# One-bank PSUM tiles from the second layer on, and the second layer's weights converted in the gated batches

## The chip, the cores and the metric

The kernel runs on one core of a Trainium2 chip. The metric is the device time of one execution in microseconds (us). A core has TensorE (PE: matmuls, with PEld for its weight loads), VectorE (DVE), ScalarE (ACT), GpSimd (POOL), and SyncE (SP), which issues nearly all DMA transfers here. Each engine works through its own instructions in the order in which they are written, and waits on semaphores where an operand is not ready or a buffer is not free.

## The reference

Three stages, each feeding the next (cut to the core):

```python
def _attn_ref(q, k, v, p):                       # batch 8, heads 8, seq 576, head_dim 64, 32 pack rows
    p_packed = sm_attn(p, k, v)
    return sm_attn(q, p_packed, p_packed)
def _moe_ref(x, w_gate, w_val, w_out, rms_g):    # 4608 tokens, 512 -> 1536 -> 512, "gated"
    xn = x / sqrt(mean(x * x) + 1e-6) * rms_g
    g = xn @ w_gate
    return silu(g) * (xn @ w_val) @ w_out
def _moe2_ref(x, w1, w2, w3, w_out):             # 512 -> 1024 -> 1024 -> 512, "second layer"
    return ((x @ w1) * (x @ w2) @ w3) @ w_out
```

q, k, v, p and rms_g arrive as fp32. The weight matrices arrive as 64-bit floats and are handed to the kernel as 64-bit words. The kernel turns each into fp32 on the core.

## The kernel before, in words

fp32 accuracy comes from splitting each operand into a high and a low part (`split`, line 54: ScalarE copies the rounded high part, VectorE or GpSimd subtracts) and adding three matmuls, high x high, high x low, low x high.

**Converting a weight.** `convert` (line 102) turns a block of 128 x 512 64-bit words into fp32: two activations on ScalarE (`c_h`, `c_y`), two VectorE instructions (`c_t`, `c_o`) and one GpSimd add. `converting` (line 116) is a generator over a list of such blocks: the first `next` issues the loads of the first few, each later `next` converts one block and issues one load. While the gated batches run three loads stand ahead, later two.

**Gated batches.** `dense_units(b)` (line 362) makes one of 8 batches: 6 groups x 2 x 2 halves x 2 units, so 48 units; a unit is 6 matmuls (line 376) into one `gv` bank. An even unit is drained by ScalarE (`th`, line 382) and VectorE (line 383), an odd one by ScalarE (`vl`, line 387); GpSimd multiplies them to `ht` (line 388), which SyncE stores to `hT_d`. There are four `gv` banks. After every eighth unit, `wb_unit` (line 330) makes the weights of the next group in an `at` tile, which ScalarE and VectorE split into `wbh` and `wbl`. `planned` (line 431) puts other work behind unit numbers: the attention of later batches (`pack`, `unpack`), and conversions. In batches 1 to 6 that is `some(ow, 2)` at units 21 and 35 (line 472), which converts the 12 blocks of `w_out` and stores them to `wo_d`.

**y stage.** `y_part(t)` (line 549) multiplies 512 tokens of `hT_d` by `w_out`: 12 units of 12 matmuls (line 558), into four banks named `at` or `gv` by turns. Beside them `together` (line 407) spreads other generators by due times: the conversions and splits of the second layer's `w3` and `w_out` and their product (`folded`, line 648), the Strassen parts of that product (`fold_parts`, line 665, stored to `w34_d`), and `layer2` (line 634). `layer2` converts four blocks of `w1` and `w2`, makes the operands of the group's seven Strassen products (seven block products in place of eight) in `group` (line 592: GpSimd adds, ScalarE and VectorE splits), and stores them to `ws_d`; then the next group. y_part 4 to 7 carry these, y_part 8 the preparation of the first token pair.

**Second layer.** Tokens go in five pairs of blocks, three of 2 x 512 and two of 2 x 384 columns (line 707). `run(p)` (line 915) first makes 8 `step`s (line 841): each is seven products of six matmuls (line 857) into four banks, `ta` to `td`, which VectorE and ScalarE combine as the products end. Then come the seven products with the folded weights (lines 941 to 951), with two sets of four banks, written in turns. Weights come from `ws_d` and `w34_d` through four buffers `w`.

**PSUM.** There are eight banks of 128 x 512 fp32. `bank()` gives one bank, tag `gv`, four buffers. `slot("at")` gives a tile of two banks, two buffers; the wide tiles are needed in the attention. `four(tag)` (line 538) returns four banks: four `gv` tiles, or the halves of two `at` slots. Even steps and the first set of products use `gv`, odd steps and the second set use `at` (lines 861 and 932). Waits are kept per tile: a matmul that starts to write one half of an `at` slot waits for readers of the other half as well.

```python
def four(tag):
    if tag == "gv":
        return [bank() for _ in range(4)]
    return [t[:, j, :] for t in (slot("at"), slot("at")) for j in range(2)]
```

Of the kernel before, what the change touches and what calls it, by code (L numbers as in the profile page):

```python
# [8 lines left out]
F32 = mybir.dt.float32  # L9
F32R = mybir.dt.float32r  # L10
I32 = mybir.dt.int32
# [13 lines left out]
NF = DFF // 128  # L25
# [7 lines left out]
def packed_attention_swiglu_bilinear(ctx: ExitStack, tc, qT, kT, v, pT, rms_g, w_gv, w_out,  # L33
                                     w1, w2, w3T, w_out2, out):
    nc = tc.nc
    PSUM = bass.MemoryType.PSUM

    const = ctx.enter_context(tc.tile_pool(name="const", bufs=1, side="left"))
    dram = ctx.enter_context(tc.tile_pool(name="dram", bufs=1, space=bass.MemoryType.DRAM))
    ps = ctx.enter_context(tc.tile_pool(name="ps", bufs=1, space=PSUM))  # L40

    hT_d = dram.tile([NF, 128, NT], F32, name="hT_d")
    wo_d = dram.tile([DFF, DM], F32, name="wo_d")
    w34_d = dram.tile([7, 128, 2, 4, 256], F32, name="w34_d")
    y_d = dram.tile([NT // TT, 128, 4, TT], F32, name="y_d")
    ws_d = [dram.tile([8, 128, 2, n, 2, 128], F32, name=f"ws{n}_d") for n in (3, 4)]

    def slot(tag):
        return ps.tile([128, 2, 512], F32, tag=tag, name=tag, bufs=2)

    def bank():
        return ps.tile([128, 512], F32, tag="gv", name="gv", bufs=4)
# [9 lines left out]
    cv = cv_ctx.enter_context(tc.tile_pool(name="cv", bufs=1, side="left"))  # L62
    cv_of = [cv]
# [52 lines left out]
    def converting(jobs, take):  # L116


        n64 = ahead64[0]
        ahead = [load64(src) for src, *_ in jobs[:n64]]  # L120
        yield
        for i, job in enumerate(jobs):
            take(ahead.pop(0), *job[1:])
            if i + n64 < len(jobs):
                ahead.append(load64(jobs[i + n64][0]))
            yield
# [4 lines left out]
    def as_f32(w):  # L131
        o = cv_of[0].tile([128, 512], F32, tag="c_o", name="c_o", bufs=c_o_bufs[0])
        convert(o, w, plain)
        return o
# [9 lines left out]
        store_later(4, out=dst, in_=as_f32(w))  # L144

    ahead64 = [3]


    pTs = att.tile([128, NC, B, NP], F32, name="pTs")
# [249 lines left out]
    def some(gen, n):  # L399
        for _ in range(n):  # L400
            yield next(gen, None)
# [5 lines left out]
    def together(main, total, *others, most=1):  # L407


        done, taken = 0.0, [0] * len(others)  # L410
        for c in main:
            done += c / total
            late = [n * (done - a) / (z - a) - taken[i] if taken[i] < n else 0.0
                    for i, (n, _, a, z) in enumerate(others)]
            for i in sorted(range(len(others)), key=lambda j: -late[j])[:most]:
                if late[i] > 0:
                    next(others[i][1], None)
                    taken[i] += 1
        for _, gen, _, _ in others:
            drain(gen)  # L420
# [37 lines left out]
            next(front[x])  # L458
    for x in "puw":
        drain(front[x])  # L460
    ow = converting([(w_out[128 * i:128 * i + 128, :], wo_d[128 * i:128 * i + 128, :]) for i in range(NF)], out_weight)

    PACK = [7, 7, 16, 31, 32, 40, 43]
    UNPACK = [0, 1, 3, 4, 6, 11, 13, 15, 17, 24, 24, 25, 31, 32, 40, 41, 42, 44]
    for b in range(B - 1):
        others = [(UNPACK, unpack(b + 1))]
        if b + 2 < B:
            others.insert(0, (PACK, pack(b + 2)))
        if b == 0:
            others.append(([1, 3, 5, 9, 12, 14, 18, 20, 22, 26, 28, 30], gvw))  # L470
        else:
            others.append(([21, 35], some(ow, 2)))
        planned(dense_units(b), *others)
    drain(ow)
    flush()
# [62 lines left out]
# [4 lines that stand above are left out]
# [41 lines left out]


    ORDER = (0, 5, 4, 1, 6, 3, 2)
    GROUPS = [(r, c) for c in range(2) for r in range(2)]
    parts = []

    def summed(w, g, n):
        parts.append(as_f32(w))  # L590

    def group(g):
        r, c = GROUPS[g]
        a11, a12, a21, a22 = parts
        parts.clear()
        to = stage[g % 2][:, :7168].rearrange("p (i j s n) -> p i j s n", i=4, j=7, s=2)

        def put(j, src, eng):
            hi, lo = (to[:, :, ORDER.index(j), s, :] for s in range(2))
            split(hi, lo, src.rearrange("p (i n) -> p i n", i=4), eng)  # L600

        put(3, a22, nc.vector)
        nc.gpsimd.tensor_tensor(out=a22, in0=a21, in1=a22, op=ALU.add)
        yield
        put(0, a11, nc.vector)
        nc.gpsimd.tensor_tensor(out=a21, in0=a11, in1=a21, op=ALU.subtract)
        nc.gpsimd.tensor_tensor(out=a11, in0=a22, in1=a11, op=ALU.subtract)
        yield
        put(4, a22, nc.vector)
        put(1, a12, nc.vector)  # L610
        nc.gpsimd.tensor_tensor(out=a12, in0=a12, in1=a11, op=ALU.subtract)
        yield
        put(6, a21, nc.vector)
        put(5, a11, nc.vector)
        yield
        put(2, a12, nc.vector)
        for i in range(4):
            store_later(2 + i, out=ws_d[0][4 * c + i, :, r], in_=to[:, i, :3].bitcast(F32))
            store_later(2 + i, out=ws_d[1][4 * c + i, :, r], in_=to[:, i, 3:].bitcast(F32))
        yield  # L620

    jobs = []
# [3 lines left out]
    for j in range(8):  # L626
        jobs.append((w3T[128 * j:128 * j + 128, 512:], w3_h[:, j], w3_l[:, j]))
    late = converting(jobs, halved)
    jobs = []
    for g, (r, c) in enumerate(GROUPS):  # L630
        for n, (w, kk) in enumerate(((w1, r), (w1, r + 2), (w2, r), (w2, r + 2))):
            jobs.append((w[128 * kk:128 * kk + 128, 512 * c:512 * c + 512], g, n))

    def layer2():
        conv = converting(jobs, summed)
        next(conv)
        yield
        for g in range(4):
            for _ in range(4):
                next(conv)  # L640
                yield
            yield from group(g)

# [66 lines left out]
    def fetch_y(p):  # L710
        if p < len(pairs):
            ys[p] = []
            row, w = pairs[p]
            for r in (row, row + w):
# [8 lines left out]

    second = layer2()
    third = fold_parts()
    together(y_part(4, "at"), 12.0, (6, some(second, 6), 0.5, 1.0), (5, some(third, 5), 0.0, 0.9))
    together(chained(y_part(5, "gv"), y_part(6, "at"), y_part(7, "gv")), 36.0, (31, second, 0.0, 0.9),
             (3, third, 0.0, 0.15),
             (1, (fetch_y(0) for _ in range(1)), 0.3, 0.4))

    flush()
# [93 lines left out]
             (3, first_w(), 0.3, 0.8))  # L825
    flush()
    wo_ctx.close()
    p3 = ctx.enter_context(tc.tile_pool(name="p3", bufs=1, side="left"))
    sides = {n: p3.tile([128, 4, TT], F32, name=n) for n in ("s11", "s21", "s12", "s22", "t1s", "t2s", "t4s")}
    OPER = {0: "s11", 4: "t1s", 5: "t2s", 1: "s21", 6: "s12", 3: "t4s", 2: "s22"}  # L830
# [10 lines left out]
    def step(p, n):  # L841
        w = width(p)
        i = LAYER[n]
        half, k = divmod(i, 4)
        xh, xl = xs[p]

        def side(name):
            return sides[name][:, k, :w]

        def prod(t, j, start):  # L850
            pos = ORDER.index(j)
            wi, pos, n = (wa, pos, 3) if pos < 3 else (wb_, pos - 3, 4)
            wi = wi[:, :512 * n].rearrange("p (r j s n) -> p r j s n", r=2, j=n, s=2)
            at = 0
            for a, x in ((0, xh), (1, xh), (0, xl)):
                for r in range(2):
                    nc.tensor.matmul(t, lhsT=wi[:, r, pos, a], rhs=x[:, j, r, :w],  # L857
                                     start=(start and at == 0), stop=(at == 5), skip_group_check=True)
                    at += 1

        ta, tb, tc_, td = (t[:, :w] for t in four("at" if n % 2 else "gv"))
        p1, u3, uc = tmp()[:, :w], tmp()[:, :w], two()
        u2, c22 = uc[:, 0, :w], uc[:, 1, :w]
        s1, s2 = (side("s21"), side("s22")) if half else (side("s11"), side("s12"))
        wa = next_w()
        prod(ta, 0, True)
        nc.scalar.activation(out=p1, in_=ta, func=AF.Copy)
        prod(tb, 5, True)
        dve(u2, tb, p1)
        prod(tc_, 4, True)  # L870
        yield
        wb_ = next_w()
        prod(ta, 1, False)
        prod(tb, 6, False)
        dve(u3, tb, p1)
        dve(c22, tc_, u3)
        yield
        prod(td, 3, True)
        dve(s1, td, u3)
        dve(s1, s1, ta, ALU.mult)  # L880
        prod(tc_, 2, False)
        dve(u2, tc_, u2)
        nc.gpsimd.tensor_tensor(out=s2, in0=u2, in1=c22, op=ALU.mult)  # L883
        if half == 0:
            diff(side("t1s"), s2, s1, nc.gpsimd)
        else:
            diff(side("t2s"), s2, side("t1s"), nc.gpsimd)
            diff(side("s12"), s2, side("s12"), nc.gpsimd)
            diff(side("t4s"), s1, side("t2s"), nc.gpsimd)
        yield  # L890
# [24 lines left out]
    def run(p):  # L915
        w = width(p)
# [12 lines left out]
        drain(diffs)  # L929
        later = splitting(p, LATER)  # L930
        sum_ = sums(p + 1)
        acc = [[t[:, :w] for t in four(tag)] for tag in ("gv", "at")]
        p1, u2, u3, c22 = [], [], [], []
        out_stores = []

# [5 lines left out]
        for a, j in enumerate(PROD):  # L941
            wi = next_w().rearrange("p (s i n) -> p s i n", s=2, i=4)
            last = {0: 1, 5: 6, 4: 2}.get(j, j) == j
            for k in range(4):
# [3 lines left out]
                for m in range(2):  # L948
                    t = acc[m][BANK[j]]
# [8 lines left out]
            for m in range(2):  # L958
                ta, tb, tc_, td = acc[m]
# [60 lines left out]
```

## Time and profile before

| | us |
|---|---|
| median of 3 runs (lowest, highest) | 1497.6 (1495.95, 1499.32) |
| the profiled execution | 1496.0 |
| its span, first to last instruction | 1494.2 |
| TensorE busy | 1360.8 (91%) |
| TensorE's share of the chain of waits that ended last | 72% of the span |
| VectorE busy | 871.6 (58%) |
| GpSimd busy | 607.0 (41%) |
| ScalarE busy | 576.5 (39%) |

Busy time is the time in which an engine executed something. Idle time stands in the groups of instructions: behind the second bar, the idle time of the engine just before these instructions, and what ended it. The stages lie in the span roughly so: attention of the first batches to 65, gated batches to 515, y stage to 866, second layer to the end.

### The profile page before, as it was taken

How to read it: one execution, taken by the hardware profiler on the slowest of the kernel's cores; microseconds unless marked ns; L12 is line 12 of the kernel's file. 1: busy time of each engine (PE TensorE's matmuls, PEld its weight loads, DVE VectorE, ACT ScalarE, POOL GpSimd, SP SyncE). 2: the span in 40 equal slices, each digit the busy share in tenths (PEclk: the TensorE clock that was granted, in tenths of full speed). 3: DMA queues.
4: the chain of work that ended last, by engine and by line, in shares of the span. 5: the costliest groups of instructions: out<-in, count | busy, mean ns of one | idle time of the engine just before them, and what ended most of it. 6: DMA issues, size and time to landing. Idle time of an engine off the chain costs nothing.

```text
span 1494.2 us, 23206 instructions
## 1 busy us (share of the span) xinstructions
PE 1360.8 (91%) x8800; PEld 1119.2 (75%) x8800; DVE 871.6 (58%) x1356; ACT 576.5 (39%) x1141; POOL 607.0 (41%) x524
## 2 busy tenths in 40 slices
PE   4579999999999999999899998998889889988888
PEld 2368888888888888888788776776667667878778
DVE  4786576676675577364786734654573447346344
ACT  3465554554556665252555410240042015014013
POOL 2455544545555622022344232452335326235233
PEclk9689999999999999999999999999999999999999
DMA  9844544433213577344899764465447545756654
GB/s 298 302 172 129 188 145 155 160 121 125 104 72 131 182 262 241 100 159 132 309 349 395 261 230 150 169 213 224 155 169 238 178 162 190 269 205 223 226 211 155
DMA packets 82080, 293.55 MB, mean 196 GB/s; under 512 B 9008, under 2 KB 14128, under 8 KB 68016
## 3 DMA queue, kind: packets, MB, share of 16 engines
q1 hardware_dynamic: 81968, 292.07, 56.4%
q8 instruction: 69, 1.13, 0.3%
q14 instruction: 43, 0.35, 0.1%
HBM read 219.68 MB, written 72.35 MB: 195 GB/s over the span
## 4 chain that ended last, share of the span: by engine, by line
PE 72%; DVE 13%; ACT 4%; DMA 3%; issue 3%; SPq 1%; POOL 0%; DVEq 0%; ACTq 0%; POOLq 0%
PE gv L376 17%; PE at L857 12%; PE gv L857 10%; PE at L558 9%; PE at L951 5%; PE gv L951 5%; PE gv L558 4%; PE gv L654 3%; DVE hr L839 3%; DVE uc L839 2%; PE at L337 2%; DMA w<-in_w_dram 1%; DMA hr<-hT_d 1%; PE at L292 1%; DVE s L839 1%
## 5 line engine op out<-in xcount | busy, mean ns | idle before, releaser
L388 POOL TENSOR_TENSOR ht<-th,vl 128x288 f32<-128x288 f32 x192 | 163.6, 861 | 166.7 <-ACT vl L387 79.3
L857 PE MATMUL at<-xh,w 128*128 128x512 f32 (+1 forms) x560 | 146.2, 383 | 56.1 <-DVE uc L839 28.1
L376 PE MATMUL gv<-ah,wbh 128*128 128x288 f32 x768 | 178.0, 313 | 7.3 <-DVE th L383 4.7
L883 POOL TENSOR_TENSOR s<-uc 128x512 f32<-128x512 f32 (+1 forms) x40 | 48.5, 1214 | 313.8 <-DVE uc L839 313.8
L376 PE MATMUL gv<-al,wbh 128*128 128x288 f32 x768 | 166.8, 298 | 0.0
L857 PEld LDWEIGHTS at<-xh,w 128*128 128x128 f32 x560 | 98.9, 189 | 90.2 <-DVE uc L839 35.7
L376 PEld LDWEIGHTS gv<-ah,wbh 128*128 128x128 f32 x768 | 122.3, 190 | 58.5 <-issue 22.8
L376 PE MATMUL gv<-ah,wbl 128*128 128x288 f32 x768 | 165.0, 296 | 0.0
L114 POOL TENSOR_TENSOR c_o<-c_o,c_y 128x512 int32<-128x512 int32 x52 | 74.4, 1431 | 173.0 <-DVE c_o L112 152.3
L857 PE MATMUL gv<-xh,w 128*128 128x512 f32 (+1 forms) x560 | 140.4, 372 | 3.4 <-DVE uc L839 2.2
L56 DVE TENSOR_TENSOR hl<-hr,hh 128x512 fp32r<-128x512 f32 x108 | 98.9, 919 | 49.5 <-ACT hh L55 49.3
L376 PEld LDWEIGHTS gv<-al,wbh 128*128 128x128 f32 x768 | 124.7, 190 | 1.0 <-DVE al L56 0.6
L376 PEld LDWEIGHTS gv<-ah,wbl 128*128 128x128 f32 x768 | 124.3, 190 | 0.0
L857 PEld LDWEIGHTS gv<-xh,w 128*128 128x128 f32 x560 | 101.4, 188 | 23.5 <-DVE uc L839 11.0
L383 DVE SCALAR_TENSOR_TENSOR th<-th,gv 128x288 f32<-128x288 f32 x192 | 84.4, 445 | 55.9 <-ACT th L382 52.1
L558 PE MATMUL at<-hl,wo_h 128*128 128x512 f32 x288 | 112.6, 391 | 2.3 <-DVE hl L56 2.3
L558 PE MATMUL at<-hh,wo_h 128*128 128x512 f32 x288 | 112.4, 390 | 0.2 <-ACT hh L55 0.2
L558 PE MATMUL at<-hh,wo_l 128*128 128x512 f32 x288 | 112.3, 390 | 0.0
L55 ACT ACTIVATE hh<-hr 128x512 fp32r<-128x512 f32 x108 | 67.5, 628 | 97.1 <-PE at L558 49.9
L387 ACT ACTIVATE vl<-gv 128x288 f32<-128x288 f32 x192 | 79.5, 414 | 62.1 <-PE gv L376 58.5
L56 DVE TENSOR_TENSOR wbl<-at,wbh 128x512 fp32r<-128x512 f32 x96 | 66.0, 687 | 61.2 <-ACT wbh L55 60.6
L951 PE MATMUL at<-sh,w 128*128 128x512 f32 (+1 forms) x280 | 83.9, 381 | 13.1 <-DVE uc L839 12.4
(148 smaller groups left out, 2828.0 us busy)
## 6 DMA issues: line engine op xcount, KB each, us to landing
w<-ws_d SPq DMA_DIRECT2D x40, 1024.0 KB, 4.8
w<-w_d SPq DMA_DIRECT2D x35, 1024.0 KB, 4.8
w<-ws_d SPq DMA_DIRECT2D x40, 768.0 KB, 4.4
hT_d<-ht SPq DMA_DIRECT2D x96, 288.0 KB, 2.6
hr<-hT_d SPq DMA_DIRECT2D x108, 256.0 KB, 5.3
w<-in_w_gv_dram SPq DMA_DIRECT2D x24, 512.0 KB, 7.2
w<-in_w_out_dram SPq DMA_DIRECT2D x20, 512.0 KB, 4.8
v<-in_v_dram SPq DMA_DIRECT2D x8, 1152.0 KB, 8.1
```

What stands on the lines that cost most here:

```text
L55: nc.scalar.activation(out=hi, in_=src, func=AF.Copy)
L56: eng_lo.tensor_tensor(out=lo, in0=src, in1=hi.bitcast(F32), op=ALU.subtract)
L114: nc.gpsimd.tensor_tensor(out=d, in0=d, in1=shape(y), op=ALU.add)
L376: nc.tensor.matmul(t[:, :HALF], lhsT=w[:, e, 256 * i + 128 * f:256 * i + 128 * f + 128], rhs=x[:, e, HALF * hf:HALF * hf + HALF], start=(n ...
L383: nc.vector.scalar_tensor_tensor(out=th, in0=th, scalar=1.0, in1=t[:, :HALF], op0=ALU.add, op1=ALU.mult)
L387: nc.scalar.activation(out=vl, in_=t[:, :HALF], func=AF.Copy, scale=0.5)
L388: nc.gpsimd.tensor_tensor(out=ht[:, hf], in0=th, in1=vl, op=ALU.mult)
L558: nc.tensor.matmul(acc[m], lhsT=w[:, kk, 128 * m:128 * m + 128], rhs=x, start=(kk == 0 and a == 0), stop=(kk == NF - 1 and a == 2))
L839: nc.vector.tensor_tensor(out=out, in0=a, in1=b, op=op)
L857: nc.tensor.matmul(t, lhsT=wi[:, r, pos, a], rhs=x[:, j, r, :w], start=(start and at == 0), stop=(at == 5), skip_group_check=True)
L883: nc.gpsimd.tensor_tensor(out=s2, in0=u2, in1=c22, op=ALU.mult)
L951: nc.tensor.matmul(t, lhsT=wi[:, s, k, 128 * m:128 * m + 128], rhs=x, start=(j in (0, 5, 4, 3) and k == 0 and n == 0), stop=(k == 3 and n ...
```

## The change

It has three parts.

1. The two-bank slots move to a pool of their own, which is closed before the second layer. In its place a pool `pt` gives four one-bank tiles `at`, and odd steps and the second set of products take these. The number of banks is the same.
2. The 16 blocks of `w1` and `w2` join the list of `w_out`'s 12. In batches 1 to 6 five places (units 9, 20, 28, 35 and 46) take the place of two, and the finished fp32 blocks are stored to a new DRAM tile `w12_d`.
3. `layer2` no longer converts. `fetch_part` loads a finished block; even groups go to the `c_o` buffers, odd groups in pairs to `w64` buffers. The seven steps of `fold_parts` all run beside y_part 4 (before: five there, the other two beside y_part 5).

```diff
+    w12_d = dram.tile([16, 128, 512], F32, name="w12_d")
+    slots_ctx = ExitStack()
+    slots = slots_ctx.enter_context(tc.tile_pool(name="slots", bufs=1, space=PSUM))
     def slot(tag):
-        return ps.tile([128, 2, 512], F32, tag=tag, name=tag, bufs=2)
+        return slots.tile([128, 2, 512], F32, tag=tag, name=tag, bufs=2)
...
-    ow = converting([(w_out[128 * i:128 * i + 128, :], wo_d[128 * i:128 * i + 128, :]) for i in range(NF)], out_weight)
+    jobs = [(w_out[128 * i:128 * i + 128, :], wo_d[128 * i:128 * i + 128, :]) for i in range(NF)]
+    for n in range(16):
+        r, c = GROUPS[n // 4]
+        w, kk = ((w1, r), (w1, r + 2), (w2, r), (w2, r + 2))[n % 4]
+        jobs.append((w[128 * kk:128 * kk + 128, 512 * c:512 * c + 512], w12_d[n]))
+    ow = converting(jobs, out_weight)
...
-            others.append(([21, 35], some(ow, 2)))
+            others.append(([9, 20, 28, 35, 46], some(ow, 5)))
...
-    def summed(w, g, n):
-        parts.append(as_f32(w))
+    def fetch_part(n):
+        if n < 16:
+            cv = cv_of[0]
+            if n // 4 % 2 == 0:
+                x = cv.tile([128, 512], F32, tag="c_o", name="c_o", bufs=4)
+            else:
+                if n % 2 == 0:
+                    two_parts.append(cv.tile([128, 512, 2], I32, tag="w64", name="w64", bufs=3))
+                x = two_parts[-1].rearrange("p n t -> p (n t)").bitcast(F32)[:, 512 * (n % 2):512 * (n % 2) + 512]
+            nc.sync.dma_start(out=x, in_=w12_d[n])
+            parts.append(x)
...
     def layer2():
-        conv = converting(jobs, summed)
-        next(conv)
+        for n in range(4):
+            fetch_part(n)
         yield
         for g in range(4):
-            for _ in range(4):
-                next(conv)
+            for n in range(4):
+                fetch_part(4 * g + 4 + n)
                 yield
             yield from group(g)
...
-    together(y_part(4, "at"), 12.0, (6, some(second, 6), 0.5, 1.0), (5, some(third, 5), 0.0, 0.9))
+    together(y_part(4, "at"), 12.0, (6, some(second, 6), 0.5, 1.0), (7, third, 0.0, 0.9))
     together(chained(y_part(5, "gv"), y_part(6, "at"), y_part(7, "gv")), 36.0, (31, second, 0.0, 0.9),
-             (3, third, 0.0, 0.15),
              (1, (fetch_y(0) for _ in range(1)), 0.3, 0.4))
...
     wo_ctx.close()
+    slots_ctx.close()
+    pt = ctx.enter_context(tc.tile_pool(name="pt", bufs=1, space=PSUM))
+
+    def banks(n):
+        if n % 2:
+            return [pt.tile([128, 512], F32, tag="at", name="at", bufs=4) for _ in range(4)]
+        return four("gv")
...
-        ta, tb, tc_, td = (t[:, :w] for t in four("at" if n % 2 else "gv"))
+        ta, tb, tc_, td = (t[:, :w] for t in banks(n))
...
-        acc = [[t[:, :w] for t in four(tag)] for tag in ("gv", "at")]
+        acc = [[t[:, :w] for t in banks(m)] for m in range(2)]
```

**TensorE, an odd step of the second layer.** Six matmuls (x1, x3, x2 in the rows) make one product, in the order `ta`, `tb`, `tc_`, then the second product into `ta`. In brackets stand the semaphores that the row waits for: DMAHW is a transfer's landing, Activation is ScalarE's count, DVE VectorE's. Before:

```order
L857 MATMUL at<-xh,w 128x512 [waits DMAHW6_49]
L857 MATMUL at<-xh,w 128x512 x3
L857 MATMUL at<-xl,w 128x512 x2
L857 MATMUL at<-xh,w 128x512 [waits Activation_49]
L857 MATMUL at<-xh,w 128x512 x3
L857 MATMUL at<-xl,w 128x512 x2
L857 MATMUL at<-xh,w 128x512 x4
L857 MATMUL at<-xl,w 128x512 x2
L857 MATMUL at<-xh,w 128x512 [waits DMAHW7_49,DVE_49]
```

The changed kernel:

```order
L879 MATMUL at<-xh,w 128x512 [waits DMAHW6_49]
L879 MATMUL at<-xh,w 128x512 x3
L879 MATMUL at<-xl,w 128x512 x2
L879 MATMUL at<-xh,w 128x512 x4
L879 MATMUL at<-xl,w 128x512 x2
L879 MATMUL at<-xh,w 128x512 x4
L879 MATMUL at<-xl,w 128x512 x2
L879 MATMUL at<-xh,w 128x512 [waits DMAHW7_49,Activation_49]
L879 MATMUL at<-xh,w 128x512 x3
L879 MATMUL at<-xl,w 128x512 x2
L879 MATMUL at<-xh,w 128x512 [waits DVE_49]
```

The wait for ScalarE's copy of `ta` has moved from the second product (into `tb`) to the fourth (into `ta` again), and the wait for VectorE's read of `tb` from the fourth to the fifth (into `tb` again).

**ScalarE, around unit 9 of a gated batch.** `e` is attention work, `th` and `vl` drain units 8, 9, 10 and 11, `wbh` splits the next group's weights, and the `th` and `vl` behind it drain units 12 and 13. Before:

```order
L188 ACTIVATE e_2429,rs<-at,nb 128x576 x2
L382 ACTIVATE th<-gv 128x288
L387 ACTIVATE vl<-gv 128x288
L382 ACTIVATE th<-gv 128x288
L387 ACTIVATE vl<-gv 128x288
L55 ACTIVATE wbh<-at 128x512 x2
L382 ACTIVATE th<-gv 128x288
L387 ACTIVATE vl<-gv 128x288
```

The changed kernel:

```order
L193 ACTIVATE e_2469,rs<-at,nb 128x576 x2
L387 ACTIVATE th<-gv 128x288
L392 ACTIVATE vl<-gv 128x288
L112 ACTIVATE c_h<-w_1981 128x512
L113 ACTIVATE c_y<-w_1981 128x512
L387 ACTIVATE th<-gv 128x288
L392 ACTIVATE vl<-gv 128x288
L59 ACTIVATE wbh<-at 128x512 x2
L387 ACTIVATE th<-gv 128x288
L392 ACTIVATE vl<-gv 128x288
```

The two activations of a conversion stand now between the draining of unit 9 and that of unit 10.

**SyncE, beside y_part 4 and the start of y_part 5.** `hr` are the rows of `hT_d` that y_part multiplies, `w_d<-stage` are stores of the folded weights, `in_w_dram` are 64-bit blocks of `w1` or `w2`. Before:

```order
L489 DMA hr<-hT_d 128x512
L99 DMA w_8505<-in_w_dram 128x1024
L99 DMA w_8507<-in_w_dram 128x1024
L489 DMA hr<-hT_d 128x512
L99 DMA w_8536<-in_w_dram 128x1024
L489 DMA hr<-hT_d 128x512 x2
L356 DMA w_d<-stage_6932 128x2048
L99 DMA w_8586<-in_w_dram 128x1024
L489 DMA hr<-hT_d 128x512
```

The changed kernel, where `c_o` and `w` are filled from `w12_d` and `ws_d` is the first store of group 0:

```order
L607 DMA c_o<-w_d 128x512 x4
L499 DMA hr<-hT_d 128x512 x2
L361 DMA w_d<-stage_7128 128x2048
L607 DMA w_8751<-w_d 128x512
L499 DMA hr<-hT_d 128x512
L607 DMA w_8751<-w_d 128x512
L499 DMA hr<-hT_d 128x512 x2
L607 DMA w_8816<-w_d 128x512 x2
...
L361 DMA ws_d<-stage_7127 128x768
```

Before, loads of 64-bit blocks are spread, two ahead of their conversion. Now the blocks of group 0 are loaded together, and those of group 1 before group 0's results are stored.

## Rows read from the trace of the kernel before

**Rows 1.** Groups by line: shapes, count | busy us, mean ns | idle before, releasers.
```profile
L857 PE MATMUL at<-xh,w 128*128 128x512 f32 (+1 forms) x560 | 146.2, 383 | 56.1 <-DVE uc L839 28.1 <-DVE s L839 14.6 <-ACT hr L867 13.5
L857 PE MATMUL gv<-xh,w 128*128 128x512 f32 (+1 forms) x560 | 140.4, 372 | 3.4 <-DVE uc L839 2.2
...
L951 PE MATMUL at<-sh,w 128*128 128x512 f32 (+1 forms) x280 | 83.9, 381 | 13.1 <-DVE uc L839 12.4
```

**Rows 2.** TensorE's timeline, two steps of 512 columns: start, us, instructions [idle before].
```profile
1002.82 1.09 PE L857 MATMUL gv<-xh,w 128*128 128x512 f32 x4
...
1012.83 1.07 PE L857 MATMUL at<-xh,w 128*128 128x512 f32 x4
...
1015.05 1.20 PE L857 MATMUL at<-xh,w 128*128 128x512 f32 x4 [0.69 <-ACT hr L867]
...
1022.30 1.21 PE L857 MATMUL at<-xh,w 128*128 128x512 f32 x4 [1.51 <-DVE uc L839]
...
1026.25 1.07 PE L857 MATMUL gv<-xh,w 128*128 128x512 f32 x4
```

**Rows 3.** TensorE's timeline, two steps of 384 columns.
```profile
1276.03 0.86 PE L857 MATMUL gv<-xh,w 128*128 128x384 f32 x4
...
1283.81 0.85 PE L857 MATMUL at<-xh,w 128*128 128x384 f32 x4
...
1294.43 0.86 PE L857 MATMUL gv<-xh,w 128*128 128x384 f32 x4
```

**Rows 4.** Busy us by stretch: PE, PEld, DVE, ACT, POOL, clock, DMA.
```profile
866.00:961.00 95.00, 82.36 (x343) 62.94 (x342) 42.72 (x57) 9.37 (x17) 30.00 (x22) 1.00 0.53 194
961.00:1003.00 42.00, 38.82 (x163) 30.12 (x162) 28.45 (x28) 21.87 (x33) 28.20 (x16) 1.00 0.60 199
```

**Rows 5.** The page's DMA issues: count, size, us to landing.
```profile
w<-ws_d SPq DMA_DIRECT2D x40, 1024.0 KB, 4.8
...
w<-ws_d SPq DMA_DIRECT2D x40, 768.0 KB, 4.4
```

**Rows 6.** TensorE's timeline, a stop in the folded products.
```profile
978.64 0.73 PE L951 MATMUL at<-sh,w 128*128 128x512 f32 x2 [1.66 <-DVE uc L839]
```

**Rows 7.** Chain of waits, y stage: start, us, what.
```profile
548.08 32.64 PE gv L558 x144
...
689.73 10.94 PE at L558 x48
...
716.97 7.00 DMA w<-in_w_dram
...
731.09 1.77 DVE hl L56
...
865.71 6.86 PE gv L857 x30
```

**Rows 8.** Busy us by stretch, around the stop in y_part 5, columns as above.
```profile
730.00:735.00 5.00, 2.12 (x6) 1.71 (x6) 5.00 (x5) 3.02 (x5) 3.63 (x3) 0.70 0.81 333
735.00:740.00 5.00, 5.00 (x15) 3.92 (x15) 4.41 (x6) 1.67 (x3) 1.48 (x2) 0.61 0.63 197
```

**Rows 9.** Groups by line: the instructions of a conversion.
```profile
L114 POOL TENSOR_TENSOR c_o<-c_o,c_y 128x512 int32<-128x512 int32 x52 | 74.4, 1431 | 173.0 <-DVE c_o L112 152.3 <-ACT hh L55 10.6 <-ACT c_h L108 9.0
...
L108 ACT ACTIVATE c_h<-w 128x512 f32<-128x512 f32 x76 | 50.7, 667 | 20.3 <-DMA w<-in_w_gv_dram 9.4 <-DMA w<-in_w_dram 4.5 <-DMA w<-in_w_out_dram 3.8
...
L111 DVE TENSOR_SCALAR c_t<-c_h 128x512 int32<-128x512 int32 x76 | 43.6, 573 | 25.1 <-ACT c_h L108 24.1
...
L112 DVE SCALAR_TENSOR_TENSOR c_o<-c_h,c_t 128x512 int32<-128x512 int32 x52 | 38.5, 740 | 1.8
```

**Rows 10.** Timeline of ScalarE and of TensorE, batch 4 at units 13 and 16.
```profile
324.71 0.42 ACT L387 ACTIVATE vl<-gv 128x288 f32<-128x288 f32 x1
...
325.18 0.54 PE L376 MATMUL gv<-ah,wbh 128*128 128x288 f32 x2 [0.29 <-ACT vl L387]
```

**Rows 11.** VectorE's low parts in the y stage: ns min/median/max, first and last start.
```profile
L56 DVE TENSOR_TENSOR hl<-hr,hh x108: 677/693/2785, 511.7 to 858.2; 128x512 fp32r<-128x512 f32 x108
```

More of the change, by code (lines that the diff above doesn't have):

```diff
@@ L146, in packed_attention_swiglu_bilinear @@
     ahead64 = [3]
+    GROUPS = [(r, c) for c in range(2) for r in range(2)]
     pTs = att.tile([128, NC, B, NP], F32, name="pTs")
@@ L585, in packed_attention_swiglu_bilinear @@
     ORDER = (0, 5, 4, 1, 6, 3, 2)
-    GROUPS = [(r, c) for c in range(2) for r in range(2)]
     parts = []
-    def summed(w, g, n):
-        parts.append(as_f32(w))
+    def fetch_part(n):
[9 more added lines that the diff above has]
+            parts.append(x)
+    two_parts = []
     def group(g):
         r, c = GROUPS[g]
-        a11, a12, a21, a22 = parts
-        parts.clear()
+        a11, a12, a21, a22 = parts[:4]
+        del parts[:4]
         to = stage[g % 2][:, :7168].rearrange("p (i j s n) -> p i j s n", i=4, j=7, s=2)
@@ L628, in packed_attention_swiglu_bilinear @@
     late = converting(jobs, halved)
[L629 to L632, printed above, removed]
     def layer2():
-        conv = converting(jobs, summed)
-        next(conv)
+        for n in range(4):
+            fetch_part(n)
         yield
         for g in range(4):
-            for _ in range(4):
-                next(conv)
+            for n in range(4):
+                fetch_part(4 * g + 4 + n)
                 yield
```

## The prediction

> **What bounds the kernel now.** I read the busy line and the 40 slices of the page first: TensorE is busy 91% of the span at nearly full granted clock, and the chain of waits is TensorE for 72%. So only TensorE's own stops can be won, or lengthened. The groups by line show where it stops [rows 1]: in line 857, the products of the second layer, the instructions that write tiles `at` stood idle 56.1 us ahead of their matmuls, the equal number that write `gv` 3.4 us; in line 951, the products with the folded weights, `at` stood 13.1 us. The two do the same arithmetic with the same operands and take turns, step by step. They differ only in the tile: a `gv` is one bank, an `at` is half of a tile of two banks, and the releasers named (the `uc`, `s` and `hr` that read the neighbour bank) are waits on the tile and not on the data.
>
> The timeline of TensorE then gives the price [rows 2]. A `gv` step of 512 columns runs from 1002.82 to 1012.83, 10.01 us; the `at` step behind it to 1026.25, 13.42 us, with stops such as 0.69 and 1.51 us. The rest of the 3.41 us is the restart, since the first four matmuls after a stop take 1.20 instead of 1.07 us and their predecessors drain first. For 384 columns [rows 3] it is 7.78 us (1276.03 to 1283.81) and 10.62 us (to 1294.43).
>
> In the stage before (y_part 4 to 8) the chain of waits runs from 689.73 to 865.71, 176.0 us [rows 7]. One y_part at full rate is 32.64 us, five are 163.2, so 12.8 us are lost there. [...]
>
> **The change part by part. One-bank tiles.** In the order of TensorE the `at` step now has the waits of a `gv` step: the wait for ScalarE has gone from the second product to the fourth, two products later than the read it waits for, and the wait for VectorE has gone from the fourth to the fifth. So I price an `at` step as a `gv` step. There are 5 pairs of token blocks with 4 `at` steps each, 3 pairs of 512 and 2 of 384 columns: 12 x 3.41 = 40.9 and 8 x 2.84 = 22.7, together 63.6 us. All of it lies on the path, since TensorE is the engine that ends last. What else must keep up: between 866 and 961 VectorE was busy 42.7, GpSimd 30.0 and ScalarE 9.4 of 95 us [rows 4]; the same work in about 81 us (14 less, four `at` steps) leaves VectorE half idle. The weights: a step loads 1024 and 768 KB, which land 4.8 and 4.4 us after issue [rows 5]; one after the other 9.2 us, which is under a `gv` step of 10.0 us and over one of 7.8, but three loads stand ahead in four buffers, so they may overlap. Nothing for it, and 16 x (9.2 - 7.78) = 22.7 us if they do not.
>
> In line 951 the `at` stops go as well: the fourth of seven products waited 1.66 us for VectorE's read of the bank beside it [rows 6]. There are about four such stops a pair, 13.1 us idle in all [rows 1], and 0.10 us more for each restart (0.73 instead of 0.63 us for two matmuls), 20 of them: 15 us. This stretch is fuller: between 961 and 1003 VectorE and GpSimd are busy 28.4 and 28.2 of 42 us [rows 4], and the splits that feed TensorE have six buffers. If they become the limit, I get perhaps 5 us of it; with the restarts fully counted 17. I take 15.
>
> **The conversions leave the y stage.** Sixteen times two activations, two VectorE instructions and one GpSimd add go, and 16 loads of 512 KB become 16 of 256 KB of finished fp32. No ScalarE instruction there waits any longer for a load issued shortly before: the order of SyncE shows the four loads of a group issued before the previous group is split. I take 9 of the 12.8 us; the rest I leave, because part of the stops late in the stage are behind stores that stay. The two fold steps that moved into y_part 4 bring two instructions on ScalarE and two on VectorE forward, with two units of `hl` ready ahead. Bounds: 0 (the stops are the loads' `hr` and stores alone, and come back there) and 12.8.
>
> **The conversions enter the gated batches.** One conversion is `c_h` and an equal `c_y` on ScalarE, 0.67 us each, `c_t` 0.57 and `c_o` 0.74 on VectorE, the add 1.43 on GpSimd [rows 9]. On a free engine nothing of this is late; on the queues the instructions behind it are. In the batches now two conversions stand, behind units 21 and 35 of 48; now five, behind 9, 20, 28, 35 and 46. The place without slack is 9: TensorE's unit 16 starts at 325.18, ended by ScalarE's `vl` that starts at 324.71 [rows 10]. The order of ScalarE shows the new pair just ahead of two `th`/`vl` and the `wbh` pair that this `vl` stands behind, so 2 x 0.67 = 1.3 us go through. The five conversions at this place are in batches 2 to 6 (batch 1 only begins the loads there): 6.5 us. At 20, 28 and 46 banks come free two or more units before they are wanted; half a microsecond in all. I take +7. Bounds: 0, if the chain closes up before unit 16; 16 x 1.33 = 21 if every conversion passes its ScalarE time on. The 16 extra stores and 16 loads of SyncE stand among the `hT_d` stores; the loads are three conversions ahead.
>
> [...] Row first: VectorE's `hl` takes 0.693 us in the median and up to 2.785 [rows 11], in the stage where GpSimd's adds run beside it. [...]
>
> **Sum.** 63.6 + 15 + 9 - 7 = 80.6 us. The profiled execution before took 1496.0 us (span 1494.2 and 1.8 around it), which gives 1415.4; the median of the three runs, 1497.6, stands 1.6 above it, so 1417; I write 1416.
>
> **Rivals.**
> - The folded products are held by VectorE and GpSimd (5 instead of 15 us): 1426. For it: 28 of 42 us busy on both engines [rows 4]. Against: every stop named there is `at` waiting for a read.
> - The y stage gives nothing: 1425. For it: TensorE's late stops there have other causes as well. Against: the load of 7.00 us and the conversion are in the chain of the largest one [rows 7].
> - The 384-column steps are held by the weights: 1416 + 23 = 1439. Against: no idle time of line 857 names a load [rows 1].
> - GpSimd's adds hold up VectorE in the batches, each for its 1.43 us, and TensorE behind it: 16 x 1.43 = 23 us, 1439. [...]
> - Each added conversion holds TensorE for its whole chain, 0.67 + 0.57 + 0.74 + 1.43 = 3.4 us, 54 instead of 7: 1463. Against: nothing TensorE needs waits for the add.
> - The new tiles wait as before (the order of banks brings other waits): 63.6 and 15 are not won, 1495, no change. Against: the order.
> - Slower: the 64-bit loads come late in the batches, behind SyncE's `hT_d` stores, and ScalarE's whole queue stands at `c_h` for a load of 7.0 us as at 717 [rows 7], then the chain of 3.4: 16 x 10.4 = 166 instead of 7, 1575. It makes the kernel slower from (63.6 + 15 + 9) / 16 = 5.5 us per conversion. Against: a load is issued three conversions ahead of its use.
>
> **How the numbers follow.** Forecast 0.70; folded products held 0.10; y stage nothing 0.08; weights 0.03; adds 0.02; whole chain 0.03; waits as before 0.02; slower 0.02. The forecast's own terms run from 63.6 + 17 + 12.8 - 0 = 93.4 (1404) to 63.6 + 12 + 4 - 14 = 66 (1431). The range 1404 to 1434 holds these and the first two rivals, both together too (1435) but for a microsecond. A measurement of this kernel can tell 0.2%, 3 us, from no change. Faster by more 0.96, within it 0.02, slower 0.02.
>
> **What would show it.** The `at` and `gv` groups of the second layer's products have the same idle time, under 5 us each, and an `at` step lasts 10.0 and 7.8 us; line 951 shows under 4 us of idle time. The stage of y_part 4 to 8 takes 165 to 170 us with no granted clock under 0.9 in a slice. The gated batches 2 to 6 are each about 1.3 us longer than now, with the extra stop at unit 16. I am wrong if steps of 384 columns show waits for `w`, if the splits `sl` become the releaser in the folded products, or if batches grow by more than 3 us each.

## The result, and the profile after

The changed kernel took 1410.7 us (median of 4 runs, 1409.9 to 1412.1) against 1498.4 us of the kernel before in the same comparison: a ratio of 0.9418, with a 95% interval of 0.9402 to 0.9434. The forecast was 1416 us and its range 1404 to 1434. The profiled execution has a span of 1408.3 us, 85.9 less than before.

The groups by line of the kernel after (shapes, count, then busy us and mean ns, then idle time ahead and who ended it) answer to [rows 1]; line 857 is now 879, and 951 is 973:

```profile
L879 PE MATMUL gv<-xh,w 128*128 128x512 f32 (+1 forms) x560 | 140.6, 372 | 3.4 <-DVE uc L861 2.8
L879 PE MATMUL at<-xh,w 128*128 128x512 f32 (+1 forms) x560 | 140.4, 372 | 3.4 <-DVE uc L861 2.5
L973 PE MATMUL at<-sh,w 128*128 128x512 f32 (+1 forms) x280 | 81.9, 374 | 0.0
```

The `at` instructions of the steps now wait as long as the `gv` ones, 3.4 us over 560 matmuls, and those of the folded products wait for nothing. TensorE's timeline (start, us, instructions, idle time before) shows two steps of 512 columns, as [rows 2], and then two of 384, as [rows 3]:

```profile
981.63 1.07 PE L879 MATMUL gv<-xh,w 128*128 128x512 f32 x4
...
990.10 1.21 PE L879 MATMUL gv<-xh,w 128*128 128x512 f32 x4 [0.15 <-DVE uc L861]
...
991.61 1.09 PE L879 MATMUL at<-xh,w 128*128 128x512 f32 x4
...
1000.11 1.20 PE L879 MATMUL at<-xh,w 128*128 128x512 f32 x4
...
1001.60 1.09 PE L879 MATMUL gv<-xh,w 128*128 128x512 f32 x4
```

```profile
1227.96 0.85 PE L879 MATMUL at<-xh,w 128*128 128x384 f32 x4
...
1235.74 0.85 PE L879 MATMUL gv<-xh,w 128*128 128x384 f32 x4
...
1243.50 0.85 PE L879 MATMUL at<-xh,w 128*128 128x384 f32 x4
```

Read start to start, a `gv` step is 9.98 us and an `at` step 9.99; at 384 columns they are 7.76 and 7.78. The stop left in a step is short and the same for both, ahead of its seventh product: 0.15 us idle and 1.21 or 1.20 us for the four matmuls instead of 1.07.

The chain of waits through the y stage, as [rows 7] (start, us, what), and the same two stretches of y_part 5 as in [rows 8] (us, busy PE, PEld, DVE, ACT, POOL, granted clock, DMA):

```profile
716.95 5.54 DMA c_o<-w_d
722.50 8.58 DMA hr<-hT_d
735.42 1.78 DVE hl L60
737.25 27.31 PE gv L568 x119
...
829.84 32.64 PE at L568 x144
```

```profile
730.00:735.00 5.00, 5.00 (x24) 4.14 (x23) 3.16 (x5) 3.82 (x7) 0.59 (x1) 1.00 1.06 418
735.00:740.00 5.00, 4.12 (x19) 3.04 (x18) 5.00 (x5) 3.11 (x6) 4.22 (x3) 1.00 1.03 417
```

The last y_part, and the two left out here before it, run at the 32.64 us of full rate, at a granted clock of 1.00. One short stop is left, in y_part 5, behind a load of `hr` that takes 8.58 us; the granted clock stays at 1.00 across it, where it was 0.61 before. The stage, from the first matmul of y_part 4 (697.86) to the first of the second layer (862.32), takes 164.5 us, 1.3 over five y_parts at full rate.

What was paid stands in the gated batches. This is batch 4 of the kernel after, at unit 9, where a conversion now stands (start, us, engine, line; rows of ScalarE, VectorE, GpSimd and TensorE):

```profile
322.95 0.41 ACT L392 ACTIVATE vl<-gv 128x288 f32<-128x288 f32 x1
...
323.24 0.69 ACT L112 ACTIVATE c_h<-w 128x512 f32<-128x512 f32 x1
323.75 0.81 POOL L393 TENSOR_TENSOR ht<-th,vl 128x288 f32<-128x288 f32 x1 [1.72 <-DVE th L388]
...
323.82 0.68 ACT L113 ACTIVATE c_y<-w 128x512 int32<-128x512 uint32 x1
323.97 0.88 DVE L115 TENSOR_SCALAR c_t<-c_h 128x512 int32<-128x512 int32 x1 [0.35 <-ACT c_h L112]
...
324.38 0.42 ACT L387 ACTIVATE th<-gv 128x288 f32<-128x288 f32 x1
...
324.88 0.69 DVE L116 SCALAR_TENSOR_TENSOR c_o<-c_h,c_t 128x512 int32<-128x512 int32 x1
...
324.96 0.62 ACT L59 ACTIVATE wbh<-at 128x512 fp32r<-128x512 f32 x1
...
325.49 0.45 DVE L388 SCALAR_TENSOR_TENSOR th<-th,gv 128x288 f32<-128x288 f32 x1
...
327.24 0.63 DVE L60 TENSOR_TENSOR wbl<-at,wbh 128x512 fp32r<-128x512 f32 x1
...
327.90 0.60 ACT L59 ACTIVATE wbh<-at 128x512 fp32r<-128x512 f32 x1 [2.32 <-DVE wbl L60]
...
328.69 0.42 ACT L392 ACTIVATE vl<-gv 128x288 f32<-128x288 f32 x1
...
329.16 0.54 PE L381 MATMUL gv<-ah,wbh 128*128 128x288 f32 x2 [1.95 <-ACT vl L392]
```

TensorE's unit 16, which waited 0.29 us before [rows 10], waits 1.95. The way there is longer than ScalarE's two conversions: the first `wbh` is done at 325.58, but `wbl` comes at 327.24, because VectorE has `c_t`, `c_o` and what queued up behind them to do first; the second `wbh` waits 2.32 us for that `wbl`, and `th` and `vl` stand behind it. This second `wbh` needs no result of that `wbl`: it reads the other half of `at` and writes the other half of its own tile. It waited in the kernel before, too, in the same batch:

```profile
323.93 0.60 ACT L55 ACTIVATE wbh<-at 128x512 fp32r<-128x512 f32 x1 [1.70 <-DVE wbl L56]
```

By the code this, too, would be a wait for a whole tile and not for data. No run gives the two halves tiles of their own, so what it costs stays open.

The span's 85.9 us come apart by stretches, each from the first matmul of one stage to that of the next in the two traces:

| stretch | before | after | difference | predicted |
|---|---|---|---|---|
| 40 steps of the second layer | 429.5 | 364.5 | -64.9 | -63.6 |
| folded products, 5 pairs | 195.7 | 177.9 | -17.8 | -15 |
| y_part 4 to 8 | 176.0 | 164.5 | -11.5 | -9 |
| gated batches 2 to 6 | 276.5 | 285.4 | +8.9 | +7 |
| all else | 416.5 | 415.9 | -0.6 | 0 |

### The profile page after: what moved, and what is told of

It is laid out like the page before. It is cut to its first block, busy times and chain, and to the rows that moved or that the text cites. A ratio compares the mean times of both kernels' runs of the same rounds, so it can differ in the third digit from the quotient of the medians.

```text
span 1408.3 us, 23274 instructions
## 1 busy us (share of the span) xinstructions
PE 1339.0 (95%) x8800; PEld 1119.5 (79%) x8800; DVE 857.2 (61%) x1356; ACT 573.7 (41%) x1141; POOL 606.5 (43%) x524
## 4 chain that ended last, share of the span: by engine, by line
PE 79%; DVE 10%; ACT 2%; issue 2%; DMA 1%; POOL 1%; SPq 0%; ACTq 0%; DVEq 0%; POOLq 0%
PE gv L381 17%; PE at L568 12%; PE gv L879 11%; PE at L879 11%; PE gv L568 7%; PE gv L973 6%; PE at L973 6%; PE gv L669 3%; PE at L342 3%; DVE uc L861 2%; DVE hr L861 2%; PE at L297 1%; DVE th L388 1%; DVE c_t L115 1%; DVE wbl L60 1%
## 5 line engine op out<-in xcount | busy, mean ns | idle before, releaser
L381 PE MATMUL gv<-ah,wbl 128*128 128x288 f32 x768 | 164.7, 296 | 0.0
L118 POOL TENSOR_TENSOR c_o<-c_o,c_y 128x512 int32<-128x512 int32 x52 | 70.7, 1360 | 172.1 <-DVE c_o L116 111.3
L879 PE MATMUL at<-xh,w 128*128 128x512 f32 (+1 forms) x560 | 140.4, 372 | 3.4 <-DVE uc L861 2.5
L60 DVE TENSOR_TENSOR wbl<-at,wbh 128x512 fp32r<-128x512 f32 x96 | 65.8, 686 | 60.9 <-ACT wbh L59 60.3
L387 ACT ACTIVATE th<-gv 128x288 f32<-128x288 f32 x192 | 79.6, 415 | 35.9 <-PE gv L381 35.8
```

Of the source, the lines that this page charges most:

```text
L60: eng_lo.tensor_tensor(out=lo, in0=src, in1=hi.bitcast(F32), op=ALU.subtract)
L118: nc.gpsimd.tensor_tensor(out=d, in0=d, in1=shape(y), op=ALU.add)
L381: nc.tensor.matmul(t[:, :HALF], lhsT=w[:, e, 256 * i + 128 * f:256 * i + 128 * f + 128], rhs=x[:, e, HALF * hf:HALF * hf + HALF], start=(n ...
L387: nc.scalar.activation(out=th, in_=t[:, :HALF], func=AF.Tanh, scale=0.5)
```

## The experiments

Seven kernels ran, each against the kernel before on the same chip (1497.1 and 1497.5 us in the two groups).

**The tiles alone.** The kernel before, with part 1 of the change and nothing of parts 2 and 3 (main lines; the new pool for `slot` is in it as well):

```diff
+    slots_ctx.close()
+    pt = ctx.enter_context(tc.tile_pool(name="pt", bufs=1, space=PSUM))
...
-        ta, tb, tc_, td = (t[:, :w] for t in four("at" if n % 2 else "gv"))
+        ta, tb, tc_, td = (t[:, :w] for t in banks(n))
...
-        acc = [[t[:, :w] for t in four(tag)] for tag in ("gv", "at")]
+        acc = [[t[:, :w] for t in banks(m)] for m in range(2)]
```

> The kernel before with one half of the change alone: the 'at' and 'gv' results of the second layer in tiles of one bank, the slots' pool closed before it; the 16 conversions stay in the y stage. Theory (waits are kept per tile, and the half tile alone made TensorE stop): the steps' and the folded products' gains come in full without the other half, 64.9 + 17.8 = 82.7 us as the two traces differ, so about 1416 us; steps of 10.0 and 7.8 us; the y stage stays at 176 us and the gated batches at 56.1 us. Rival (part of the second layer's gain comes from the conversions, for instance from other places of the weights in memory or from a clock that is not lowered late in the y stage): the steps or the products keep some of their stops, and the time is 1430 us or more.

Measured: 1411.0 us, ratio 0.9428 (0.9415 to 0.9440), some 86 us off: a little more than the 82.7 expected, and the changed kernel's time within the intervals. The groups by line of this kernel have the steps' `at` stops gone:

```profile
L868 PE MATMUL at<-xh,w 128*128 128x512 f32 (+1 forms) x560 | 140.2, 372 | 3.4 <-DVE uc L850 1.6
```

Its second layer takes 544.6 us to the end of the span, where the kernel before takes 628.7: 84.1 of the 86. Its y stage keeps 175.3 us, batches 3 to 5 keep 56.1. So the tiles alone win what the whole change wins, to within 3 us, and they need nothing of the conversions.

**The new pool, with the old tile size.** The kernel with the tiles alone, but two banks to a tile again:

```diff
-            return [pt.tile([128, 512], F32, tag="at", name="at", bufs=4) for _ in range(4)]
+            two = [pt.tile([128, 2, 512], F32, tag="at", name="at", bufs=2) for _ in range(2)]
+            return [t[:, i] for t in two for i in range(2)]
```

> The kernel with one half of the change alone (1411.0 us), with its 'at' results of the second layer back in tiles of two banks, but in the new pool: same memory, same order of instructions, only the tile's size differs. Theory (a wait for a half is a wait for the whole tile): steps of 13.4 and 10.6 us, products of 43.6 us, and the time of the kernel before, 1497 us, within 3 us. Rival (the new pool's place in memory or its other turn of buffers did it): 1411 us. In between: each has a part.

Measured: 1495.4 us, ratio 0.999 (0.9978 to 1.0003). The stops are back to the tenth, with the same three releasers as in [rows 1]:

```profile
L869 PE MATMUL at<-xh,w 128*128 128x512 f32 (+1 forms) x560 | 146.0, 382 | 56.1 <-DVE uc L851 28.0 <-DVE s L851 14.6 <-ACT hr L879 13.5
...
L963 PE MATMUL at<-sh,w 128*128 128x512 f32 (+1 forms) x280 | 83.9, 381 | 13.0 <-DVE uc L851 12.4
```

Neither the pool nor the order of the banks had a part that shows in 3 us; the size of a tile did, and so what a wait covers. The gaps repeated step by step, and no PSUM was added to close them: the same four banks, as four tiles instead of two, took the idle time ahead of the steps' `at` matmuls from 56.1 to 3.4 us.

**The conversions alone.** The changed kernel, with part 1 undone (main lines):

```diff
-        ta, tb, tc_, td = (t[:, :w] for t in banks(n))
+        ta, tb, tc_, td = (t[:, :w] for t in four("at" if n % 2 else "gv"))
...
-        acc = [[t[:, :w] for t in banks(m)] for m in range(2)]
+        acc = [[t[:, :w] for t in four(tag)] for tag in ("gv", "at")]
```

> The changed kernel with the two-bank tiles put back: only the conversions are moved into the gated batches. Theory: the batches lengthen by 8.8 us, as in the changed kernel, the y stage shortens by 11.5, so 2.7 us are won and the time is about 1495.7 us; the second layer's stops stay (steps of 13.4 and about 10.6 us at full clock). Rival (the move was worth more because of something it does for the second layer): 1490 us or less. Rival (the move costs what it gives): 1498 us or more.

Measured: 1495.6 us, ratio 0.999 (0.9979 to 1.0002): 1.5 us won, between 3.1 won and 0.3 lost. The y stage takes 164.7 us and batch 4 57.9, as in the changed kernel, and the second layer stops as before:

```profile
L868 PE MATMUL at<-xh,w 128*128 128x512 f32 (+1 forms) x560 | 146.5, 383 | 56.2 <-DVE uc L850 28.0
```

So parts 2 and 3 give 11 us in the y stage and pay back about 9 in the batches; by themselves they can't be told from no change.

**The fold's parts as before.** The changed kernel, with the division of the folding undone:

```diff
-    together(y_part(4, "at"), 12.0, (6, some(second, 6), 0.5, 1.0), (7, third, 0.0, 0.9))
+    together(y_part(4, "at"), 12.0, (6, some(second, 6), 0.5, 1.0), (5, some(third, 5), 0.0, 0.9))
...
+             (3, third, 0.0, 0.15),
```

> The changed kernel with the parts of the folding divided as in the kernel before (five in y_part 4, three in y_parts 5 to 7) instead of all in y_part 4; the 16 conversions stay in the batches. Theory (the y stage's gain is the conversions' removal): y stage between 163.5 and 166.5 us and the time within 2 us of the changed kernel's 1410.7. Rival (the other division brought the gain): y_part 5 goes back to about 40 us, and the time is about 1417 us.

Measured: 1412.6 us, ratio 0.9438 (0.9416 to 0.9460). The y stage, 697.39 to 863.53, takes 166.1 us, 1.7 more than in the changed kernel. Its chain of waits shows y_part 5 no longer than there, and a stop in the last part instead, behind a load of `hr`:

```profile
736.42 27.31 PE gv L568 x119
...
...
835.54 6.25 DMA hr<-hT_d
844.30 2.91 DVE hl L60
847.26 16.43 PE at L568 x71
```

So by the traces about 10 of the 11.5 us of the y stage are the conversions' and 1.7 the fold's; the times, 1.9 us apart with overlapping intervals, don't tell the fold's from nothing.

**The conversion at unit 9 in two halves.** The changed kernel; `begin` issues the load and ScalarE's `c_h` and `c_y`, `finish` VectorE's `c_t` and `c_o`, GpSimd's add and the store:

```diff
-            others.append(([9, 20, 28, 35, 46], some(ow, 5)))
+            others.append(([9], begin()))
+            others.append(([24], finish()))
+            others.append(([20, 28, 35, 46], some(ow, 4)))
```

> The changed kernel with the conversion at unit 9 of the gated batches cut in two: ScalarE's two operations (c_h, c_y) stay at unit 9, the two of VectorE (c_t, c_o) and GpSimd's addition go to unit 24; the four other conversions stay. Theory of the prediction (ScalarE's two operations, 1.3 us, are what reaches TensorE at unit 16): the stop there stays about 1.9 us, batches 2 to 5 stay near 57.5 us, and the time is about 1409 us. Rival (VectorE's share, a wait of 0.35 us plus 0.88 and 0.61 us, is the longer way to the weights of the next group): the stop falls back to about 0.6 us, batches 2 to 5 to 56.1 to 56.4 us, and the time is about 1403 us.

Measured: 1414.7 us, ratio 0.9460 (0.9446 to 0.9474), slower than the changed kernel, which neither theory had. The timeline of batch 4 (rows of TensorE, SyncE and VectorE) tells why: the stop at unit 16 did shrink, but a new one came at unit 40, behind a conversion that waits for its buffer:

```profile
332.95 0.54 PE L407 MATMUL gv<-ah,wbh 128*128 128x288 f32 x2 [1.28 <-ACT vl L418]
...
353.26 0.33 SPq L86 DMA_DIRECT2D v<-in_v_dram  x1
353.69 0.38 SPq L387 DMA_DIRECT2D w_d<-c_o  x1
...
361.41 0.69 DVE L122 SCALAR_TENSOR_TENSOR c_o<-c_h,c_t 128x512 int32<-128x512 int32 x1 [2.13 <-DMA w_d<-c_o]
...
362.02 0.68 DVE L60 TENSOR_TENSOR wbl<-at,wbh 128x512 fp32r<-128x512 f32 x1
...
363.99 0.53 PE L407 MATMUL gv<-ah,wbh 128*128 128x288 f32 x2 [1.99 <-ACT vl L418]
```

The half at unit 24 has its store let go four steps later, and there it stands in SyncE's queue behind a load of `v`: it is issued at 353.69, and `c_o` at unit 35, which finds neither of its two buffers free, goes on at 361.41, with `wbl` behind it. That is the experiment's own cost. Batch 5, the only one of batches 2 to 5 without the stop at unit 40, takes 57.2 us, the others 60.3 to 60.8. Unit 16 can still be read: 1.28 us, between 0.29 and 1.95.

**The two halves, with earlier stores.** The same, with the conversions' stores on a list of their own (`held_w`), counted down beside the other and let go after two steps:

```diff
-            store_later(4, out=dst, in_=o)
+            held_w.append([2, dict(out=dst, in_=o)])
```

> As the run with the two halves (ScalarE's operations of the first conversion at unit 9, VectorE's and GpSimd's at unit 24), but the conversions' stores are let go after two steps instead of four, so that the conversion at unit 35 no longer waits for the buffer of the one at unit 24 (2.13 us there, and a stop of 2.3 us at unit 40). Theory (of the 1.67 us that the changed kernel's stop at unit 16 has grown, ScalarE's two operations are 0.95 and VectorE's share is 0.68): the stop at unit 16 stays at 1.6 us, the one at unit 40 goes, batches 2 to 5 are about 57.1 us, and the time is about 1407 us, between the changed kernel and the one with other places (1401.6). Rival (the stop at unit 40 was of the halves and not of the store): it stays, and the time is 1413 us or more.

Measured: 1405.8 us, ratio 0.9389 (0.9371 to 0.9407). The store of unit 24's block is now issued at 342.17, ahead of the load of `v` at 347.15, and the stop at unit 40 is gone from batches 2 to 4; at unit 16 of batch 4 stands

```profile
326.86 0.54 PE L412 MATMUL gv<-ah,wbh 128*128 128x288 f32 x2 [1.28 <-ACT vl L423]
```

and batches 3 to 5 take 57.1 us, between 56.1 and 57.8. So of the 1.66 us by which unit 16 waits longer in the changed kernel, 0.99 stay with ScalarE's two operations, and 0.67 go with the other half, VectorE's two operations and GpSimd's add.

**Five places without unit 9.** The changed kernel with no conversion at unit 9, its stores let go after two steps as above:

```diff
-            others.append(([9, 20, 28, 35, 46], some(ow, 5)))
+            others.append(([20, 24, 28, 31, 46], some(ow, 5)))
```

> The changed kernel with the five conversions of a gated batch at units 20, 24, 28, 31 and 46 instead of 9, 20, 28, 35 and 46, their stores let go after two steps instead of four so that two buffers do. Theory (the cost is the place at unit 9, ahead of the weights that unit 16 needs): batches 2 to 5 go back to about 56.1 us, batch 6 to 51.6, and the time is about 1402 us. Rival (five conversions cost the batch some 1.7 us wherever they stand): 1410 us, with the stop at another unit. Rival (closer places wait for each other's buffers and queue up): batches of 59 us and 1416 us.

Measured: 1401.6 us, ratio 0.9368 (0.9355 to 0.9381), whose interval lies below the changed kernel's: this version is faster than the changed kernel, too. Unit 16 of batch 4 is back at its old wait,

```profile
326.13 0.53 PE L386 MATMUL gv<-ah,wbh 128*128 128x288 f32 x2 [0.33 <-ACT vl L397]
```

and batches 2 to 6 take 57.2, 56.1, 56.6, 56.0 and 52.0 us, 1.4 over the kernel before in all, where the changed kernel is 8.9 over. The earlier stores alone are not the cause, since the run before this one has them and keeps 1.28 us at unit 16. Five conversions fit into a batch nearly free; the place at unit 9 was most of the cost.

## Why the prediction was right

The sum was 80.6 us, and the spans differ by 85.9. Of the 5.3 us between them 2.8 are the folded products', 1.3 the steps' and 0.6 lie outside the predicted stretches. The move of the conversions came out 2.5 us better in the y stage and 1.9 worse in the batches; that these two errors nearly cancel is luck. The slow end of the range took 12, 4 and 14 us for the products, the y stage and the batches, which the prediction doesn't work out; measured were 17.8, 11.5 and 8.9.

**The steps.** An `at` step priced as a `gv` step, 63.6 us; measured 64.9. It is an `at` step of 3.44 and 2.96 us saved instead of 3.41 and 2.84, since the steps taken for the price were the two neighbours shown and not the mean. At 384 columns the mean also holds the last step of the kernel before, of 11.6 us, which ends at a lowered clock (granted 0.83 from 1450 to 1460). The reason, a wait on the tile and not on the data, is shown by the two runs that differ in the tile's size alone, 1411 and 1495 us.

**The folded products.** 15 us taken, 17.8 measured. The 15 were 13.1 of idle time and 20 restarts of 0.10; the trace before has three stops a pair, 15 in all, and a stop cost more. The first pair went from 43.57 to 39.35 us, 4.2, of which 3.2 was idle time, so a stop there cost some 0.3 us beyond its idle time. The figure given with full restarts, 17, was the nearer. VectorE and GpSimd, busy 28 of 42 us before [rows 4], did not become the limit; in the changed kernel TensorE is busy 39.3 of 39.3 us with VectorE at 27.9 and GpSimd at 29.2:

```profile
942.30:981.60 39.30, 39.30 (x169) 31.62 (x168) 27.86 (x31) 22.17 (x33) 29.23 (x16) 1.00 0.64 209
```

**The weights.** Priced at nothing, rightly, though single loads got slower: the profile's page after has 5.0 and 5.1 us to landing where [rows 5] have 4.8 and 4.4. No step waits for one: the only stop in a step is the short one ahead of its seventh product.

```profile
w<-ws_d SPq DMA_DIRECT2D x40, 1024.0 KB, 5.0
...
w<-ws_d SPq DMA_DIRECT2D x40, 768.0 KB, 5.1
```

**The y stage.** 9 of 12.8 us taken, by estimate, 11.5 measured. The largest loss was that of y_part 5, behind the load of 7.00 us [rows 7] and its conversion, with the granted clock of 0.61 [rows 8]: it took 40.57 us, and now takes 33.86. What I left for stops "behind stores that stay" was too much: only y_part 5 still loses, 1.2 us. The stage came out half a microsecond under the 165 to 170 us named.

**The batches.** +7 taken, +8.9 measured, and here a step was wrong in its working though near in its sum. Place and stop were as said: unit 9, felt at unit 16. But I let ScalarE's 1.3 us through whole and VectorE's work through as nothing. Of ScalarE's 1.3 us 0.99 came through, and 0.67 of the other half on top. These are there because `c_t` waits 0.35 us for `c_h` with the next `th` queued behind it, is then held by GpSimd (0.88 us instead of 0.42), and `wbl`, which I had not put on the path, stands behind all of it. Batch 6 lengthened most, by 2.5 us: it has stops of 0.89 us at unit 16 and of 1.11 at unit 40, a place that the prediction did not name.

**GpSimd and VectorE.** In the sum the adds cost GpSimd alone. At unit 9 it is less the add that holds VectorE than `ht`: `c_t` at 323.97 lasts 0.88 us, where its median is 0.42, and ends 0.29 us after `ht`, which runs to 324.56. The rival at 1439, a full 1.43 us for each add, fell, since the batches lengthened by 8.9 us in all. But in batch 6 GpSimd seems to reach TensorE through VectorE, at unit 40, behind a conversion at unit 35, where one stood before, too:

```profile
465.96 1.27 DVE L115 TENSOR_SCALAR c_t<-c_h 128x512 int32<-128x512 int32 x1 [0.91 <-ACT c_h L112]
466.13 1.77 POOL L393 TENSOR_TENSOR ht<-th,vl 128x288 f32<-128x288 f32 x2
467.26 1.18 DVE L116 SCALAR_TENSOR_TENSOR c_o<-c_h,c_t 128x512 int32<-128x512 int32 x1
...
470.34 0.53 PE L381 MATMUL gv<-ah,wbh 128*128 128x288 f32 x2 [1.11 <-ACT vl L392]
```

In batch 6 of the kernel before, the conversion at unit 35 has 0.55 and 0.69 us for these two, and unit 40 does not stop. With that conversion moved to unit 31, in the run without unit 9, the stop at unit 40 of batch 6 is 0.21 us.

The rivals that ended slower or at no change needed late 64-bit loads or waits that stay; the conversion in batch 4's rows waits for no load, and the groups of the second layer show no such wait. Unit 9 stood in the prediction as a cost, and not as one that other places avoid.

## What to carry to other kernels

When two groups do the same arithmetic and one stops where the other doesn't, compare the tiles before the engines: here a tile that holds two banks made the writer of one wait for the reader of the other, 56.1 us in the steps against 3.4 with one bank to a tile. Work moved into a stage with idle engines was nearly free at most of its places here and dear at one or two (batches 2 to 6 grew by 8.9 us, and by 1.4 without unit 9), so look for the instruction there that TensorE waits for last, and follow it back through every queue, not the longest one alone. Before an experiment moves a producer, count the buffers until its store lets one go, and see what stands ahead of that store in its queue.

## What the runs showed that was not expected

GpSimd holds up `c_t`, which reads a single tile. The tile's row in the trace after (min, median, max ns) has a tail:

```profile
L115 DVE TENSOR_SCALAR c_t<-c_h x76: 384/422/1320, 13.9 to 670.2; 128x512 int32<-128x512 int32 x76
```

Fifty of the 76 run beside no GpSimd instruction and take 0.38 to 0.43 us, and so do three that are under way when one starts. Twenty-three start while one is running, and each of them ends 0.28 or 0.29 us after a GpSimd instruction has ended, however long that took; here it is one of 1.42 us, which ends at 115.09, and `c_t` at 115.38:

```profile
113.67 1.42 POOL L303 TENSOR_TENSOR sq<-sq 128x576 f32<-128x576 f32 x1
...
114.06 1.32 DVE L115 TENSOR_SCALAR c_t<-c_h 128x512 int32<-128x512 int32 x1
```

So the end of such a `c_t` follows the end of a GpSimd instruction by 0.28 or 0.29 us, whatever the length of either. What holds it until then, these traces do not show.
